# Pair 0's operands through a landing tile, key signs before the last sum, and bits first in each pair's first score tile

## The chip, the cores and the metric

The kernel runs on one core of a Trainium2 chip. The metric is the device time of one execution in microseconds (us); the median of several runs is compared. TensorE (PE) multiplies, VectorE (DVE) and ScalarE (ACT) do elementwise work, GpSimd (POOL) and SyncE (SP) mainly issue DMAs here.

## The reference

Bucketed attention over 4 batches x 8 heads, 768 positions, 64 dimensions, and then a gated feed-forward block. A query sees only keys whose six hash bits equal its own:

```python
q_bits = (np.einsum('bhsd,dk->bhsk', q, proj) > 0)      # k_bits likewise
mask = q_bucket[:, :, :, None] == k_bucket[:, :, None, :]
scores = np.where(mask, scale * np.matmul(q, k.transpose(0, 1, 3, 2)), -1000000000.0)
attn = softmax(scores)                                  # over keys, sum + 1e-09
x = matmul(attn, v)   -> (B*S, H*D)
out = (silu(x @ w_gate) * (x @ w_val)) @ w_out
```

The weights of the feed-forward block are doubles (they are read as pairs of 32-bit words); everything else is fp32.

## The kernel before

The attention stage works on 16 pairs of heads. A pair has 12 units: two halves of 384 queries by six blocks of 128 keys. For a unit, `products` (T) multiplies the transposed keys with the transposed queries of both heads in fp32, two passes each, and `mark` adds a product of bit patterns in bf16 to the same PSUM tile and then lets ScalarE take Exp of it into a ring of 12 weight tiles (A). The bit product is what masks: where two hash codes differ, the score falls far below. After the 12 units come, on TensorE, the sums of the pair before (`total`, L581), the hash products of the next pair (`hash_blocks`, L430), and `attend` (L545), which multiplies the weights with v for all 12 units. TensorE issues strictly in this written order, and so does every other engine: nothing is moved by a scheduler.

The bits of the next pair are made while this pair attends. ScalarE takes the sign of each hash product (`sign`, L435) in the order query half 0, query half 1, key half 0, key half 1; between the query and the key signs stands the copy of the row of sums (L586), which a small DMA on SP (L588) reads. `spread_q` (L447) is a DMA on the POOL queue that copies the query bits to the second head's rows. `spread_k` (L444) does the same for keys with two VectorE operations, each times a mask. Key signs and `spread_k` are put into a list `rest`, which the main loop empties at the end of the pair.

VectorE's order in a pair: the two transposes of the next pair's keys and queries (L458), then sums of the weights in `add` (L563, L567, L570 for the first half, the same for the second), then `spread_k`, the normalisation of the pair before last (L610), a reciprocal (L594) that waits for the small DMA, splits of finished outputs (L291, L296), and the conversion of feed-forward weights in pieces. A piece costs ScalarE three and VectorE five operations (L139 to L168). `PACE` says how many pieces are begun in each pair, 24 in all; the others follow in the feed-forward stage.

Pair 0 has no pair before it, so `start_first` prepares it by itself. Queries come on SP's queue and keys on ScalarE's, each in four DMAs (two heads, two halves), straight into the tile `raw`, whose rows hold both heads side by side, so that a run in memory is 64 numbers, 256 B. TensorE transposes (L468), ScalarE and VectorE copy the result out of PSUM (L472, L475). Nine matmuls with zeros (L367) keep TensorE busy until then. VectorE's copies of the hash matrix (L394) wait for two DMAs of `proj` on POOL.

PSUM is a ring of four tiles of two banks; each unit, each `joint` tile (sums and hashes) and each `av` tile takes the next one.

The feed-forward stage starts when the attention stage has issued, and takes the rest of the time.

Of the kernel before, what the change touches and what calls it, by code (L numbers as in the profile page):

```python
# [8 lines left out]
FP32 = mybir.dt.float32  # L9
# [10 lines left out]
def kernel(  # L20
# [20 lines left out]
    nc = tc.nc  # L41
    PSUM = bass.MemoryType.PSUM
    B, H, S, D = q.shape
# [37 lines left out]
    def two_banks(name):  # L81
        return pp.tile([P, 2, 512], FP32, tag="pp", name=name)
# [6 lines left out]
    def finish(todo):  # L89
        while todo:  # L90
            todo.pop(0)()
# [210 lines left out]
    def attention(scope):  # L302
# [9 lines left out]
        def fetch(n, name, queue, half=None):  # L312
            b, pr = pairs[n]
            if name == "v":
                t = raws["v", n] = raw.tile([P, 2, NCH, D], FP32, tag="vraw", name="vraw")
                queue.dma_start(
                    t.rearrange("p h c d -> p h (c d)"),
                    v[b, 2 * pr : 2 * pr + 2].rearrange("h (p c) d -> p h (c d)", c=NCH),
                )
                return  # L320
            src = q if name == "q" else k
            if not half:
                raws[name, n] = raw.tile([P, NCH, 2, D], FP32, tag=name + "raw", name=name + "raw",
                                         bufs=1)
            t = raws[name, n]
            if n == 0:
                cs = slice(half * CH, (half + 1) * CH)
                for h in range(2):
                    queue.dma_start(t[:, cs, h, :],  # L329
                                    src[b, 2 * pr + h].rearrange("(p c) d -> p c d", c=NCH)[:, cs, :])  # L330
                return
            blocks = t.rearrange("p c a b -> p (c a b)").rearrange(
                "p (c a d) -> p c a d", a=P // BLOCK, d=BLOCK)
            for h in range(2):
                for x in range(D // BLOCK):
                    at = h * D + x * BLOCK
                    queue.dma_start(
                        blocks[at : at + BLOCK],
                        src[b, 2 * pr + h][:, x * BLOCK : (x + 1) * BLOCK].rearrange(
                            "(a p c) d -> p c a d", c=NCH, p=BLOCK))  # L340

        def load(n, names):
            if n < len(pairs):
                for name in names:
                    fetch(n, name, nc.sync)

        two_proj = fixed.tile([P, NBITS], FP32, tag="proj", name="proj")
        for o in (0, D):
            nc.gpsimd.dma_start(two_proj[o : o + D, :], proj[:, :])
# [13 lines left out]
        for t in (sides["k", 0], sides["q", 0], sides["q", 1]):  # L363
            nc.vector.memset(t, 0.0)
        idle = two_banks("idle")
        for i in range(9):
            nc.tensor.matmul(idle[:, i % 2], zeros[:, 0:P], zeros[:, 0:512], start=True, stop=True)  # L367

        HR = 16
# [34 lines left out]
            twos.append(t)  # L404
        ring = [t[:, i] for t in twos for i in range(2)]

        for n, name in ((1, "k"), (1, "q"), (0, "v"), (1, "v")):
            fetch(n, name, nc.sync)
        load_words(3, nc.sync)

        T = {}
        bits = {}

# [8 lines left out]
        def front(n):  # L422
            bits["q", n] = sides["q", n % 2]
            bits["k", n] = sides["k", n % 2]
            low, high = slice(0, BLOCK), slice(D, D + BLOCK)

            def hash_blocks(todo):
                tile_ = joint(n - 2)[:, 1]
                for i, (name, half) in enumerate(todo):
                    nc.tensor.matmul(tile_[i * BLOCK : (i + 1) * BLOCK, 0:HQ], hash_w,  # L430
                                     T[name, n][:, half * HQ : (half + 1) * HQ],
                                     start=True, stop=True)

                def sign(i, name, half, to=low, **how):
                    nc.scalar.activation(bits[name, n][to, half * HQ : (half + 1) * HQ],  # L435
                                         tile_[i * BLOCK : (i + 1) * BLOCK, 0:HQ], AF.Sign,
                                         **(how or {"bias": nudge[name]}))

                return [lambda i=i, at=at, **how: sign(i, *at, **how) for i, at in enumerate(todo)]

            def spread_k(times, cols=slice(0, S)):
                b = bits["k", n][:, cols]
                for to, by in ((high, times[1]), (low, times[0])):
                    nc.vector.tensor_scalar(b[to], b[low], scalar1=by, scalar2=None, op0=ALU.mult)  # L444

            def spread_q():
                nc.gpsimd.dma_start(bits["q", n][high], bits["q", n][low])  # L447

            def hash_next(todo):
                q0, q1, *ks = hash_blocks(todo)  # L450
                q0()
                q1()
                spread_q()
                return ks + [lambda: spread_k(times_k)]

            def transpose_blocks(name):
                T[name, n] = opnd.tile([P, S], FP32, tag=name + "T", name=name + "T")
                nc.vector.transpose(T[name, n], raws[name, n].rearrange("p c h d -> p (c h d)"))  # L458

            def start_first():  # L460
                for half in range(2):
                    cols = slice(half * HQ, (half + 1) * HQ)
                    for name in "kq":
                        if not half:
                            T[name, n] = opnd.tile([P, S], FP32, tag=name + "T", name=name + "T")
                        ps = two_banks("tps")[:, 0]
                        for i in range(CH):
                            nc.tensor.transpose(ps[:, i * P : (i + 1) * P],  # L468
                                                raws[name, n][:, half * CH + i].rearrange("p h d -> p (h d)"),
                                                ident)  # L470
                        if name == "k":
                            nc.scalar.activation(T[name, n][:, cols], ps[:, 0:HQ], AF.Copy,  # L472
                                                 scale=2 / OFF)
                        else:
                            nc.vector.tensor_copy(T[name, n][:, cols], ps[:, 0:HQ])  # L475

                def both_heads(sign, name, half):
                    cols = slice(half * HQ, (half + 1) * HQ)
                    sign()
                    if name == "k":  # L480
                        spread_k(mask, cols)
                    else:
                        nc.vector.tensor_copy(bits["q", n][high, cols], bits["q", n][low, cols])

                products(0)
                todo = [("k", 0), ("q", 0), ("k", 1), ("q", 1)]
                signs = hash_blocks(todo)
                for i in range(2):
                    both_heads(signs[i], *todo[i])
                products(1)  # L490
                products(2)
                for i in range(3):
                    mark(i)
                    if i < 2:
                        both_heads(signs[2 + i], *todo[2 + i])

            order = [("q", 0), ("q", 1), ("k", 0), ("k", 1)]
            if n:
                return [lambda name=name: transpose_blocks(name) for name in "kq"] + [
                    lambda: hash_next(order)]  # L500
            return start_first()
# [10 lines left out]

        banks_of = {}

        def product(u, x, start):
            n, half, c = units[u]
            qs = slice(half * HQ, (half + 1) * HQ)
            ks = slice(c * P, (c + 1) * P)
            for h in range(2):
                rows = slice(h * D, (h + 1) * D)  # L520
                nc.tensor.matmul(banks_of[u][:, h], x["k", n][rows, ks], x["q", n][rows, qs],  # L521
                                 start=start, stop=not start)

        def products(u):
            banks_of[u] = two_banks("sc")[:, :, 0:HQ]
            product(u, T, True)

        def mark(u):
            product(u, bits, False)
            nc.scalar.activation(weights(u)[:, :, 0:HQ], banks_of.pop(u), AF.Exp,  # L530
                                 scale=SCALE * (1.0 if units[u][0] else OFF / 2))

        def score(u):
            products(u)
            mark(u)

        def attend(u):
            n, half, c = units[u]
# [84 lines left out]
                    rest.extend(f for f in steps.pop(0)() or [] if f)  # L623

        front(0)
        steps = front(1)
        last = []
        PACE = [2] * 4 + [1] * 4 + [2, 1] * 4
        splits = []
        later = []  # L630
        TURN = 5
        for n in range(len(pairs)):
# [5 lines left out]
            for i in range(2 * NCH):  # L638
                if u + i > 2:
                    score(u + i)  # L640
                if n == 0 and i == TURN:
                    prepare_pair(2)
                if i % NCH:
                    add(u + i)
                if i == (2 if n else TURN):
                    load(n + 2, "qk")
            row = total(n - 1) if n else None
            if more:
                prepare_pair(1)
            if row:  # L650
                row()
            finish(rest)
            finish(last)
            while waiting:
                last.append(waiting.pop(0)())
# [277 lines left out]
```

## Time and profile before

| what | value |
|---|---|
| median of three runs | 912.94 us (912.37 to 913.92) |
| the profiled execution | 913.47 us, span 911.4 us |
| mean granted TensorE clock | 0.999 |
| busy PE, DVE, ACT, POOL | 904.0, 666.6, 448.0, 97.0 us |
| start until the steady run of pair 0 | 0 to 13.4 us |
| attention, pairs 1 to 15 | 28.9 to 318.6 us |
| feed-forward | 318.6 to 911.4 us |
| one regular pair | 19.23 us |

The span runs from the first to the last instruction; the device time holds some 2 us more around it. All times below are from the span's start. A line of a timeline gives start, length, engine, source line, operation, what it writes and reads, shapes and count, and in brackets how long the engine had been idle and on what it waited.

### The profile page before, as it was taken

The numbers are of one execution on the slowest core, as the hardware profiler recorded it, in microseconds if no ns is written. First come the engines' busy times: TensorE is split into PE (matmuls) and PEld (weight loads), VectorE is DVE, ScalarE is ACT, GpSimd is POOL, SyncE is SP. The second block draws the span as 40 slices with busy tenths as digits, with TensorE's granted clock in tenths as the row PEclk, the third lists the DMA queues.
The fourth block names the chain that finished last, engine by engine and source line by source line (L and its number), as shares of the span: only waits on it lengthen the run. The fifth ranks groups of instructions, "written<-read, shape, count | busy, mean of one in ns | idle before, by whom it ended". The sixth has DMA issues, their size and how long they took to land.

```text
span 911.4 us, 12610 instructions
## 1 busy us (share of the span) xinstructions
PE 904.0 (99%) x4795; PEld 636.1 (70%) x4795; DVE 666.6 (73%) x774; ACT 448.0 (49%) x604; POOL 97.0 (11%) x193
## 2 busy tenths in 40 slices
PE   8999999999999999999999999999999999999998
PEld 4444444444444488888888888888888888888886
DVE  5889999989988968779785855465668754474746
ACT  6889888878888655452414243331313233413220
POOL 1111111011111120000100000101000100001000
PEclk9999999999999999999999999999999999999999
DMA  7777788787897599685756562444434642525332
GB/s 180 132 188 199 195 214 192 162 193 208 224 227 211 200 382 331 218 289 207 297 177 238 202 259 104 173 139 157 155 139 151 242 147 97 207 70 208 104 139 93
DMA packets 145579, 174.25 MB, mean 191 GB/s; under 512 B 106496, under 2 KB 115200, under 8 KB 145520
## 3 DMA queue, kind: packets, MB, share of 16 engines
q0 software_dynamic: 22864, 116.36, 36.4%
q1 hardware_dynamic: 121056, 56.71, 24.9%
q8 instruction: 38, 0.62, 0.3%
q10 hardware_dynamic: 1600, 0.39, 0.2%
q14 instruction: 21, 0.17, 0.1%
HBM read 133.17 MB, written 39.42 MB: 189 GB/s over the span
## 4 chain that ended last, share of the span: by engine, by line
PE 97%; DVE 1%; DMA 1%; ACTq 0%; issue 0%; ACT 0%; DVEq 0%
PE a L690 29%; PE o L690 22%; PE sc L521 17%; PE n L690 14%; PE av L545 13%; PE joint L581 1%; PE joint L430 1%; DMA vraw<-in_v_dram 1%; DMA kraw<-in_k_dram 0%; DVE both L567 0%; DVE both L563 0%; DVE acc L570 0%; ACTq L329 0%; DVE kb L444 0%; DVE kT L458 0%
## 5 line engine op out<-in xcount | busy, mean ns | idle before, releaser
L690 PE MATMUL a<-xparts,ring 128*128 128x512 f32 x1152 | 273.0, 389 | 0.0
L690 PEld LDWEIGHTS a<-xparts,ring 128*128 128x128 f32 x1152 | 216.1, 188 | 45.5 <-issue 0.6
L690 PE MATMUL o<-ring,hid 128*128 128x512 f32 (+1 forms) x870 | 199.1, 388 | 0.0
L690 PEld LDWEIGHTS o<-ring,hid 128*128 128x128 f32 x870 | 162.1, 188 | 35.2 <-DVE hid L745 1.0
L521 PE MATMUL sc<-qT,kT 64*128 64x384 f32 x768 | 156.9, 487 | 0.6 <-ACT A L530 0.6
L530 ACT ACTIVATE A<-sc 128x768 f32<-128x768 f32 x192 | 151.8, 815 | 7.5 <-PE sc L521 4.2
L690 PE MATMUL n<-xparts,ring 128*128 128x512 f32 x576 | 142.2, 389 | 0.0
L545 PE MATMUL av<-A,vraw 128*64 128x386 f32 (+1 forms) x768 | 127.7, 488 | 0.0
L690 PEld LDWEIGHTS n<-xparts,ring 128*128 128x128 f32 x576 | 108.1, 188 | 22.5
L735 DVE TENSOR_TENSOR v<-v,n 128x1024 f32<-128x1024 f32 x36 | 44.0, 1221 | 98.7 <-PE n L690 98.0
L248 POOL DMA_DIRECT2D ring<-ram x108 | 56.9, 529 | 499.9 <-PE n L690 328.4
L545 PEld LDWEIGHTS av<-A,vraw 128*64 128x64 f32 x768 | 53.7, 136 | 73.3 <-issue 63.4
L521 PEld LDWEIGHTS sc<-qT,kT 64*128 64x128 f32 x768 | 67.6, 187 | 48.5 <-issue 46.3
L729 ACT ACTIVATE g<-a 128x1024 f32<-128x1024 f32 x36 | 37.0, 1027 | 130.8 <-PE a L690 126.6
L740 ACT ACTIVATE hid<-v 128x1024 fp32r<-128x1024 f32 x36 | 38.2, 1062 | 114.5 <-DVE v L739 114.5
L737 ACT ACTIVATE g<-g 128x1024 f32<-128x1024 f32 x36 | 38.2, 1062 | 86.0 <-DVE g L735 86.0
L792 DVE TENSOR_TENSOR o<-o 128x512 f32<-128x512 f32 x92 | 63.0, 687 | 20.6 <-ACT o L786 18.2
L735 DVE TENSOR_TENSOR g<-g,n 128x1024 f32<-128x1024 f32 x36 | 43.8, 1217 | 32.7 <-PE n L690 32.7
L521 PE MATMUL sc<-qb,kb 64*128 64x384 bf16 x384 | 63.4, 323 | 1.1 <-DVE kb L444 1.1
L567 DVE TENSOR_TENSOR both<-both,A 128x1536 f32<-128x1536 f32 x32 | 56.2, 1757 | 3.2
L563 DVE SCALAR_TENSOR_TENSOR both<-A 128x1536 f32<-128x1536 f32 x32 | 55.7, 1741 | 3.5 <-ACT A L530 1.9
L743 DVE SCALAR_TENSOR_TENSOR hid<-hid,v 128x1024 fp32r<-128x1024 f32 x36 | 44.0, 1224 | 19.2 <-ACT hid L740 19.1
(79 smaller groups left out, 696.8 us busy)
## 6 DMA issues: line engine op xcount, KB each, us to landing
ring<-ram POOLq DMA_DIRECT2D x108, 768.0 KB, 5.1
ram<-stage POOLq DMA_DIRECT2D x23, 768.0 KB, 5.6
ram<-stage SPq DMA_DIRECT2D x13, 768.0 KB
qraw<-in_q_dram SPq DMA_DIRECT2D x64, 96.0 KB
vraw<-in_v_dram SPq DMA_DIRECT2D x16, 384.0 KB
out_dram<-o SPq DMA_DIRECT2D x23, 256.0 KB
kraw<-in_k_dram SPq DMA_DIRECT2D x60, 96.0 KB
r<-sums SPq DMA_DIRECT2D x30, 192.0 KB
```

The costliest lines, as they stand in the source:

```text
L248: nc.gpsimd.dma_start(t.bitcast(FP32), ram[at].bitcast(FP32))
L521: nc.tensor.matmul(banks_of[u][:, h], x["k", n][rows, ks], x["q", n][rows, qs], start=start, stop=not start)
L530: nc.scalar.activation(weights(u)[:, :, 0:HQ], banks_of.pop(u), AF.Exp, scale=SCALE * (1.0 if units[u][0] else OFF / 2))
L545: nc.tensor.matmul(ps[h * D : (h + 1) * D, 0:width], raws["v", n][:, h, c, :], a[:, h, 0:width], start=c == 0, stop=c == NCH - 1)
L563: nc.vector.scalar_tensor_tensor(out=t, in0=first, scalar=S * EPS / P / 2, in1=now, op0=ALU.add, op1=ALU.add)
L567: nc.vector.tensor_tensor(t, t, now, op=ALU.add)
L690: nc.tensor.matmul(ps, w, x, start=start, stop=stop)
L735: nc.vector.tensor_tensor(two(z), two(z), n_, op=ALU.subtract)
L737: nc.scalar.activation(z, z, AF.Silu)
L740: nc.scalar.activation(h, val, AF.Copy, scale=TOWARD / STEP)
L743: nc.vector.scalar_tensor_tensor(out=l, in0=h.bitcast(FP32), scalar=-STEP, in1=val, op0=ALU.mult, op1=ALU.add)
L792: nc.vector.tensor_tensor(accs[c], accs[c], t[:, 1], op=ALU.subtract)
```

## The change

Four parts.

1. Pair 0's keys and queries are loaded in memory order into a tile `landing` (runs of 768 B, both heads in one DMA, two DMAs each in place of four) and copied from there to the `raw` tiles, keys by ScalarE and queries by VectorE, in front of the transposes. The landing tile takes the place in memory of `both`, which is used first later. Seven idle matmuls stand where nine stood.
2. The loads of pair 1, of the first two v tiles and of three weight pieces stand after `front(0)` in the code instead of ahead of it, in the same order on SP.
3. All four signs and both spreads go into `rest`, keys first. The main loop runs the first three of them (two key signs and `spread_k`) ahead of the pair's last `add`, then that `add`, then the query signs and `spread_q`, and only then the row copy.
4. In the first unit of pairs 1 to 15 the bit product opens the PSUM tile and the fp32 product closes it. In all other units the order stays. `PACE` is 2 in pairs 0 to 2, 1 in pairs 3 to 7, then 2, 1, 2, 1, 2, 2, 2, 1 (before: 2 in pairs 0 to 3, 1 in 4 to 7, then 2, 1 four times).

```diff
             if n == 0:
-                cs = slice(half * CH, (half + 1) * CH)
-                for h in range(2):
-                    queue.dma_start(t[:, cs, h, :],
-                                    src[b, 2 * pr + h].rearrange("(p c) d -> p c d", c=NCH)[:, cs, :])
+                at = slice(half * CH * D, (half + 1) * CH * D)
+                queue.dma_start(
+                    landing[name].rearrange("p h c d -> p h (c d)")[:, :, at],
+                    src[b, 2 * pr : 2 * pr + 2].rearrange("h (p c) d -> p h (c d)", c=NCH)[:, :, at])
                 return
...
+        room = att.tile([P, 2, 2, HQ], FP32, tag="both", name="landing", bufs=1)
+        landing = {name: room[:, i].rearrange("p x q -> p (x q)").rearrange(
+            "p (h c d) -> p h c d", h=2, d=D) for i, name in enumerate("qk")}
...
-        for i in range(9):
+        for i in range(7):
             nc.tensor.matmul(idle[:, i % 2], zeros[:, 0:P], zeros[:, 0:512], start=True, stop=True)
...
             def hash_next(todo):
-                q0, q1, *ks = hash_blocks(todo)
-                q0()
-                q1()
-                spread_q()
-                return ks + [lambda: spread_k(times_k)]
+                q0, q1, k0, k1 = hash_blocks(todo)
+                return [k0, k1, lambda: spread_k(times_k), q0, q1, spread_q]
...
+                        here = slice(half * CH, (half + 1) * CH)
+                        (nc.scalar.copy if name == "k" else nc.vector.tensor_copy)(
+                            raws[name, n].rearrange("p c h d -> p h c d")[:, :, here],
+                            landing[name][:, :, here])
                         ps = two_banks("tps")[:, 0]
...
         def score(u):
-            products(u)
-            mark(u)
+            if u % (2 * NCH):
+                products(u)
+                mark(u)
+            else:
+                banks_of[u] = two_banks("sc")[:, :, 0:HQ]
+                product(u, bits, True, False)
+                product(u, T, False, True)
+                mark(u, False)
...
-        PACE = [2] * 4 + [1] * 4 + [2, 1] * 4
+        PACE = [2] * 3 + [1] * 5 + [2, 1] * 2 + [2] * 3 + [1]
...
-                if i % NCH:
+                if i % NCH and i < 2 * NCH - 1:
                     add(u + i)
...
             if more:
                 prepare_pair(1)
+            for _ in range(3):
+                if rest:
+                    rest.pop(0)()
+            add(u + 2 * NCH - 1)
+            finish(rest)
             if row:
                 row()
-            finish(rest)
             finish(last)
```

More of the change, by code (lines that the diff above doesn't have):

```diff
@@ L405, in attention @@
         ring = [t[:, i] for t in twos for i in range(2)]
-        for n, name in ((1, "k"), (1, "q"), (0, "v"), (1, "v")):
-            fetch(n, name, nc.sync)
-        load_words(3, nc.sync)
         T = {}
@@ L513, in attention, with product @@
         banks_of = {}
-        def product(u, x, start):
+        def product(u, x, start, stop):
             n, half, c = units[u]
@@ L521, in product, with mark @@
                 nc.tensor.matmul(banks_of[u][:, h], x["k", n][rows, ks], x["q", n][rows, qs],
-                                 start=start, stop=not start)
+                                 start=start, stop=stop)
         def products(u):
             banks_of[u] = two_banks("sc")[:, :, 0:HQ]
-            product(u, T, True)
-        def mark(u):
-            product(u, bits, False)
+            product(u, T, True, False)
+        def mark(u, last=True):
+            if last:
+                product(u, bits, False, True)
             nc.scalar.activation(weights(u)[:, :, 0:HQ], banks_of.pop(u), AF.Exp,
@@ L625, in attention @@
         front(0)
+        for n, name in ((1, "k"), (1, "q"), (0, "v"), (1, "v")):
+            fetch(n, name, nc.sync)
+        load_words(3, nc.sync)
         steps = front(1)
         last = []
-        PACE = [2] * 4 + [1] * 4 + [2, 1] * 4
+        PACE = [2] * 3 + [1] * 5 + [2, 1] * 2 + [2] * 3 + [1]
         splits = []
```

## The prediction

> **What bounds the kernel now.** I read the busy shares first, then the table by stage, the chain of waits, and last the timelines of three places where the chain leaves TensorE or loses time on it: one pair opening, the one long stall, and the start.
>
> The page's first part, then the table of stages (start to end, length, busy time of PE, PEld, DVE, ACT, POOL, clock, DMA):
>
> ```profile
> PE 904.0 (99%) x4795; PEld 636.1 (70%) x4795; DVE 666.6 (73%) x774; ACT 448.0 (49%) x604; POOL 97.0 (11%) x193
> ...
> 0.00:13.40 13.40, 10.48 (x53) 4.43 (x53) 5.17 (x16) 5.59 (x8) 2.71 (x23) 1.00 0.58 105
> 28.90:318.56 289.66, 288.93 (x2041) 138.19 (x2041) 263.63 (x315) 237.85 (x362) 37.41 (x62) 1.00 0.78 197
> 318.56:911.40 592.84, 589.08 (x2599) 486.31 (x2598) 384.73 (x431) 192.40 (x216) 56.38 (x107) 1.00 0.53 189
> ```
>
> TensorE is the bound everywhere except in the first 13.4 us. The feed-forward stage (592.84 us) is not touched by the change. So what can be won is in 0 to 13.4 and in the gaps of 0.73 us in 28.9 to 318.6, plus what a busy PE hides: matmuls that issue later than they could.
>
> The chain of waits (start, length, what) shows a regular pair of 19.23 us (9.89 scores, about 1.4 sums and hashes, 7.91 attend) and one irregular place:
>
> ```profile
> 67.36 9.89 PE sc L521 x72
> 78.68 7.91 PE av L545 x48
> 86.59 3.43 PE sc L521 x24
> 90.01 4.79 DMA vraw<-in_v_dram
> 97.11 1.65 DVE both L563
> 98.85 1.77 DVE both L567
> 100.72 0.97 DVE acc L570
> 101.78 1.77 DVE both L563
> 103.64 1.77 DVE both L567
> 107.50 9.22 PE sc L521 x68
> ```
>
> From the opening at 86.52 to the one at 145.29, three pairs, it is 58.77 us where 3 x 19.23 = 57.69 would do, so 1.08 us is lost around pair 5. The timeline of VectorE and TensorE there says on what:
>
> ```profile
> 103.64 1.76 DVE L567 TENSOR_TENSOR both<-both,A 128x1536 f32<-128x1536 f32 x1
> 105.51 0.96 DVE L570 TENSOR_TENSOR acc<-both 128x768 f32<-128x768 f32 x1
> 106.50 0.85 DVE L444 TENSOR_SCALAR kb<-kb,columns 32x768 bf16<-32x768 bf16 x2
> ...
> 107.50 0.34 PE L521 MATMUL sc<-qb,kb 64*128 64x384 bf16 x2 [0.73 <-DVE kb L444]
> ```
>
> The spreading of the key signs (L444) stands behind the last sum of the pair (L567, L570), and in this pair VectorE is late.
>
> A regular opening and the unit after it (TensorE's timeline, pair 2):
>
> ```profile
> 48.06 0.92 PE L521 MATMUL sc<-qT,kT 64*128 64x384 f32 x4
> 48.81 0.33 PE L521 MATMUL sc<-qb,kb 64*128 64x384 bf16 x2
> 48.97 0.81 PE L521 MATMUL sc<-qT,kT 64*128 64x384 f32 x4
> 49.62 0.33 PE L521 MATMUL sc<-qb,kb 64*128 64x384 bf16 x2
> ```
>
> A later unit takes 0.81 us (48.97 to 49.78); the first takes 0.91[...].
>
> The start (TensorE's and VectorE's timelines):
>
> ```profile
> 5.76 0.17 DVE L394 COPY hash<-proj 64x6 f32<-64x6 f32 x1 [0.64 <-DMA proj<-in_proj_dram]
> ...
> 6.62 0.52 PE L468 MATMUL tps<-ident,kraw 128*128 128x128 f32 x3 [0.65 <-DMA kraw<-in_k_dram]
> 7.40 0.92 PE L521 MATMUL sc<-qT,kT 64*128 64x384 f32 x4
> ```
>
> The second half of the keys holds the transposes to 6.62, and the first scores issue at 7.40. From there to 13.33 everything is one chain of hash, signs, spread, Exp, so a shift at 7.40 reaches the end in full.
>
> [...]94 ns for kb against 187 for kT. [...]the idle matmuls issue 0.43 us apart for 512 columns, while later 384 columns take 0.16. [...]the trace has 421 ns for 512 elements from SBUF (L153) and 558 for 384 from PSUM (L475). [...]the packet records here take 18 ns for 256 B, 46 for 1024 B, 65 for 1536 B.
>
> **The change part by part.**
>
> *Opening with bits.* In pairs 1 to 15 the first unit issues bits, T, T instead of T, T, bits. Today the first T pass takes 48.06 to 48.48, 0.42 us where later ones take 0.32: 105 ns of exposed loading. Bits that came after a stall (107.50) were followed by T at 107.66, 0.16 to 0.17 where 0.16 is regular: some 10 ns exposed. Gain 15 x 0.095 = 1.43 us. Unit 1's T then follows T, whose pass of 0.32 hides a load of 0.19. Bounds: 1.2 if half the exposure of a fast load shows, 1.5 if none.
>
> *Key signs ahead of the last sum.* L444 moves in front of L567 and L570, so it comes 1.86 + 0.99 = 2.85 us sooner when VectorE is late. In pair 4 it would end near 104.5, before the opening at 105.85, and the 1.08 us go. The price is that VectorE waits for the key signs where it is early: they leave ScalarE 12.64 us after the opening (first sign at 11.46, two of 0.59), against 11.1 for the end of the second L563. So the last sum ends some 1.2 us later in pairs 1 and 2 (38.12 + 1.86 = 39.98, signs at 41.5). Behind it are L610, the reciprocal, the pieces and the next transposes. In pair 3 the lag meets one piece less (PACE 1 for 2: 0.42 + 0.69 + 0.69 = 1.8 us), and the later pairs run at 18.0 us of VectorE work (13.1 of rows that every pair has, 3.1 for one piece, 1.8 for a split) per 19.1. I walked this through all pairs with these rows: L444 ends 2.5 to 5 us before each opening, the transposes before each hash; at the end two pieces in pair 13 add 3.1 us of VectorE, and the sums of pair 15 still end about 1.7 us before their total. Cost 0; up to 1.5 if that last slack is wrong.
>
> *Query signs last.* Their DMA (L447, POOL) is issued after both key signs, 1.18 us later, and with bits first it is needed 0.75 sooner. Its landing:
>
> ```profile
> DMA to landing us min/median/max: 2.1/3.6/5.3
> ```
>
> Taken one by one (issue plus landing plus 1.18 against the opening): pair 5, 99.53 + 4.9 + 1.18 = 105.6 against 105.85; pair 6, 119.66 + 5.3 + 1.18 = 126.1 against 125.99; pair 13, 0.65 us spare; the rest 0.9 to 3.0. Cost 0.1, bounds 0 and 0.6. The row copy (L586) also goes 1.2 us later, but the few DMA behind it on SP waits for key loads in nearly every pair anyway (row done at 61.2, reciprocal at 66.5).
>
> *Landing tile.* Keys and queries of pair 0 come in 768 B runs, 4 DMAs for 8. Packets: 3072 x 18 ns / 16 = 3.5 us before; 1024 at about 37 ns (between 18 and 46) / 16 = 2.4 after, and the bytes are the same, so the second halves land about 1.1 us sooner, near 5.4 for 6.5. Added: two ScalarE copies (between 0.48 of L586 and 0.67 of L139; 0.55) and two VectorE copies. No row shows that copy; 0.25 (L483, bf16) to 0.56 (L475, PSUM); by L153 less 128 elements, 0.36. The VectorE copies stand behind the two hash copies (L394), which wait for proj, today to 5.76. With t for that moment: query copy t + 0.13 to 0.49, transposes to t + 1.1, qT to 1.69, second copy to 1.99, transposes from 2.05, scores at t + 2.49. Equal to today's 7.40 at t = 4.91. The second proj DMA was issued at 1.91 and shares the engines with the 3072 packets; with fewer I take t = 5.2 (between 4.9, close behind the first at 4.96, and 5.76 unchanged): cost 0.3, bounds 0 and 0.85, plus 0.4 if the copy runs at the slow rate; and a gain of up to 0.6 if proj lands at 4.3. ScalarE's side ends earlier: copy by 4.6, kT by 5.6, second copy by 6.2, its transposes by 6.8, before the second query ones.
>
> *Two idle matmuls less.* They end at 4.28 for 5.14. Cost 0 if the clock still opens near 5.1.
>
> *Fetches after front(0), PACE.* The pair-1 loads still wait for the transposes (kraw issued at 7.18); 24 pieces in both. 0.
>
> Sum: -1.43 - 1.08 + 0.1 + 0.3 = -2.11. The profiled execution took 913.47 us (span 911.40), 0.53 above the median 912.94; it becomes 911.36, and the median 910.8.
>
> **The rivals.**
>
> 1. *The start eats the gain.* proj unchanged at 5.76 and slow copies: +0.85 to +1.25, total -1.2 to -1.6: 911.5. For: VectorE's order puts proj in front. Against: less traffic. Chance 0.13.
> 2. *The start gains.* t near 4.3: total -3.0: 909.9. Chance 0.14.
> 3. [...]Only 3.0 us of idle matmuls, then a gap while the query copy waits; transposes, first scores and hashes (about 0.33 + 0.33 + 0.85 + 0.65 us) would take twice that: +2.2, about 913.0.[...] Chance 0.07.
> 4. *Slower: query bits late at every opening.* If L447's landing grows by x, the pairs pay what exceeds their slack. By the list above x = 0.9 costs 2.1 and cancels the gain; x = 1.5 costs 5.3, giving 916. For: the landing already varies from 2.1 to 5.3, and POOL's DMA now starts beside VectorE's last sum. Against: same engines and traffic. Chance 0.18.
>
> **How the numbers follow.** The forecast's own case has 0.48, 910.2 to 911.5. About 0.2%, 1.8 us, is what a measurement of this kernel can tell from no change, so the border is 911.1: seven tenths of the own case and rival 2 lie below (0.34 + 0.14 = 0.48); the rest of the own case, rivals 1 and 3 and a little of 4 are within (0.14 + 0.13 + 0.07 + 0.02 = 0.36); rival 4 gives slower 0.16. The range leaves out most of rival 4 and the best of rival 2: 909.6 to 913.5.
>
> **What would show it.** Right: unit 0 of a pair takes 0.82 us; no wait of TensorE on L444 around 105; a pair is 19.13 us; first scores near 7.7. Wrong: openings that wait for the qb DMA, a start beyond 8.2, or a score matmul at half clock after 6 us; any of these adds up to more than the 2.1 us.

## The result, and the profile after

| | median us | runs |
|---|---|---|
| before | 912.54 | 5 (912.09 to 913.92) |
| after | 927.49 | 5 (926.38 to 928.38) |

The ratio is 1.0162, 95% interval 1.0147 to 1.0177. The change costs 1.6%, 14.8 us by the ratio, where 910.8 us were forecast. The profiled execution took 927.25 us, its span 925.5 (before: 913.47 and 911.4).

The chain of waits of the changed kernel first, in a stretch of regular pairs (start, length, what):

```profile
88.82 9.80 PE sc L521 x72
98.62 0.78 PE joint L588 x8
99.40 0.65 PE joint L429 x8
100.05 7.91 PE av L552 x48
107.96 9.80 PE sc L521 x72
```

From 88.82 to 107.96 is one pair: 19.14 us for 19.23, with 9.80 us of scores for 9.89. No step of VectorE stands in this part of the chain any more. So two parts of the change do what they were meant to do. TensorE's and VectorE's timelines of the same place:

```profile
107.89 0.34 PE L521 MATMUL sc<-qb,kb 64*128 64x384 bf16 x2
108.06 1.45 PE L521 MATMUL sc<-qT,kT 64*128 64x384 f32 x8
```

```profile
103.53 0.86 DVE L443 TENSOR_SCALAR kb<-kb,columns 32x768 bf16<-32x768 bf16 x2
104.31 1.74 DVE L574 TENSOR_TENSOR both<-both,A 128x1536 f32<-128x1536 f32 x1
```

The bits open without a wait, the first fp32 product follows 0.17 us after them, and the key bits are spread at 103.53, ahead of the last sum.

The loss is elsewhere. The table by stage (start to end, length, busy time of PE, PEld, DVE, ACT, POOL, clock, DMA share, GB/s):

```profile
0.00:15.90 15.90, 11.62 (x51) 4.39 (x51) 5.80 (x18) 6.47 (x10) 2.72 (x23) 0.89 0.55 119
31.42:280.10 248.68, 248.68 (x1768) 118.68 (x1768) 224.97 (x270) 207.08 (x314) 29.50 (x49) 1.00 0.77 192
280.10:332.40 52.30, 43.24 (x274) 20.04 (x272) 38.01 (x46) 30.93 (x48) 8.00 (x13) 0.90 0.51 182
332.40:925.50 593.10, 589.12 (x2602) 486.43 (x2598) 384.67 (x431) 192.44 (x216) 56.39 (x107) 1.00 0.53 189
```

Row two is 13 pairs in which TensorE is busy all the time. The feed-forward stage is 593.1 us as before. Rows one and three hold the loss. The start ends 2.5 us later (the fourth unit's bits issue at 15.85 for 13.33). The stretch of the last two pairs takes 52.3 us, where the same stretch of before took 38.6:

```profile
279.90:318.49 38.59, 38.59 (x274) 18.30 (x272) 35.53 (x43) 29.76 (x45) 6.66 (x11) 1.00 0.65 223
```

Of the 13.7 us between them TensorE stands idle for 9.1; in the other 4.6 it is busy with the same 274 matmuls, at a mean clock of 0.90. With 1.3 us won by the openings of the 13 pairs and 1.0 by the stall that is gone, the sum is 2.5 - 2.3 + 13.7 + 0.2 for the tail = 14.1, the difference of the spans.

What TensorE waits for in row three, on its timeline:

```profile
288.32 1.65 PE L521 MATMUL sc<-qT,kT 64*128 64x384 f32 x4 [5.62 <-ACT xT L559]
312.56 1.65 PE L521 MATMUL sc<-qT,kT 64*128 64x384 f32 x4 [3.43 <-ACT xT L559]
```

Both stalls fall at the opening of a pair (14 and 15). xT is ScalarE's copy of the finished output out of PSUM (0.79 us); the page's row of these matmuls has 9.1 us of waiting for it in the whole execution, and these two are all of it. ScalarE's timeline tells why it is late here:

```profile
276.75 0.69 ACT L140 ACTIVATE words<-words 128x512 int32<-128x512 uint16 x1
286.31 0.66 ACT L139 ACTIVATE stage<-words 128x512 f32<-128x512 f32 x1 [8.87 <-DMA ram<-stage]
...
287.48 0.79 ACT L559 COPY xT<-av 128x768 f32<-128x768 f32 x1
```

In front of the copy stands L139, the first step of a piece of feed-forward weights, and it waits 8.87 us for a DMA. In before the same engine at the same place goes through:

```profile
280.01 0.17 ACT L551 ACTIVATE e<-av 128x1 f32<-128x1 f32 x1 [2.83 <-PE av L545]
280.08 0.79 ACT L552 COPY xT<-av 128x768 f32<-128x768 f32 x1
```

There ScalarE waits for TensorE, as it should. The chain of waits of the changed kernel gives the DMA's own history:

```profile
275.92 3.15 DMA few<-row
279.10 0.23 DVE few L601
...
279.90 0.69 DVE stage L168
...
281.16 5.04 DMA ram<-stage
...
286.31 0.66 ACT stage L139
...
287.58 0.69 ACT xT L559
```

VectorE finishes an older piece (L168) in this very pair, behind a reciprocal that waits for a small DMA, and the write-out of that piece lands at 286.20. Only then is its tile free for L139.

The reason lies in how the tiles are shared. `stage` tiles are two in turn, and a tile holds two pieces, 2k and 2k+1. Pieces begun in pair n are scaled by ScalarE in pair n, but written out by VectorE's steps in pair n+1, and in the code ScalarE's part of a pair (`begin_pieces`) stands ahead of VectorE's (`advance_pieces`). An even piece i opens a new tile; that tile last held pieces i-4 and i-3. So piece i-3 has to be begun in pair n-2 at the latest. The old `PACE` keeps to this everywhere. The new one begins 19 and 20 in pair 13 and 21 and 22 in pair 14, while 17 was begun in pair 12 and 19 in pair 13: pieces 20 and 22 break the rule, and the stalls are at the openings that follow pairs 13 and 14.

The start, on VectorE's and TensorE's timelines:

```profile
5.53 0.36 DVE L397 COPY hash<-proj 64x6 f32<-64x6 f32 x2 [1.10 <-DMA proj<-in_proj_dram]
5.92 0.36 DVE L463 COPY qraw<-landing 128x384 f32<-128x384 f32 x1
```

```profile
6.34 0.55 PE L468 MATMUL tps<-ident,qraw 128*128 128x128 f32 x3 [0.99 <-DVE qraw L463]
7.89 0.88 PE L468 MATMUL tps<-ident,qraw 128*128 128x128 f32 x3 [0.68 <-DVE qraw L463]
8.70 1.65 PE L521 MATMUL sc<-qT,kT 64*128 64x384 f32 x4
```

The hash copies wait for `proj` and are done at 5.89; the query copy stands behind them. Then three transposes take 0.88 us where three took 0.55, and four score matmuls 1.65 for 0.92: the clock is at half from 7.89 to 11.30.

### The profile page after: what moved, and what is told of

Its sections match the earlier page's. It is cut to its first block, busy times and chain, and to the rows that moved or that the text cites. A ratio compares the mean times of both kernels' runs of the same rounds, so it can differ in the third digit from the quotient of the medians.

```text
span 925.5 us, 12551 instructions
## 1 busy us (share of the span) xinstructions
PE 908.2 (98%) x4793; PEld 636.8 (69%) x4793; DVE 666.6 (72%) x776; ACT 449.3 (49%) x606; POOL 97.1 (10%) x193
## 4 chain that ended last, share of the span: by engine, by line
PE 95%; DMA 1%; ACT 1%; issue 1%; DVE 1%; DVEq 0%; ACTq 0%; POOLq 0%
PE a L704 28%; PE o L704 21%; PE sc L521 17%; PE n L704 14%; PE av L552 12%; PE joint L588 1%; PE joint L429 1%; DMA ram<-stage 1%; DMA proj<-in_proj_dram 0%; DMA few<-row 0%; ACT kb L434 0%; ACT stage L139 0%; ACT words L140 0%; DVE kb L443 0%; PE tps L468 0%
## 5 line engine op out<-in xcount | busy, mean ns | idle before, releaser
L521 PEld LDWEIGHTS sc<-qT,kT 64*128 64x128 f32 x768 | 70.0, 192 | 52.9 <-issue 34.0
```

## The experiments

Twelve kernels, in three groups, each beside runs of before of its own (medians 913.16, 913.01 and 912.34 us). A ratio is to these, and so kernels of two groups are best compared by their ratios; differences of medians are named as such. Theory S says that the turn-over of the stage tiles (their reuse for later pieces) makes the two stalls, L that too many pieces late in the stage do.

**1. a_regroup: the changed kernel, pieces shared out to tiles one place later from piece 9 on.** `PACE`, and with it the work of every engine in every pair, stays.

```diff
-        if i // 2 not in stages:
-            stages[i // 2] = stagep.tile([P, 2, 3, PIECE], FP32, tag="stage", name="stage")
-        staged[i] = st = stages[i // 2][:, i % 2]
+        at = i if i < 9 else i + 1
+        if at // 2 not in stages:
+            stages[at // 2] = stagep.tile([P, 2, 3, PIECE], FP32, tag="stage", name="stage")
+        staged[i] = st = stages[at // 2][:, at % 2]
```

> The changed kernel with its own PACE; only the grouping of the weight pieces two to a stage tile is moved by one from piece 8 on, so that no tile's two pieces begin in different pairs where PACE is 2, 2, 2. Theory S (the stalls at the openings of pairs 14 and 15 come from a stage tile shared by two pieces that were begun in different pairs: ScalarE's L139 waits for a write-out that VectorE can only issue in the same pair): both stalls go, 927.5 - 13.9 = 913.6. Theory L (three pairs with two pieces each in a row are too much work or traffic for VectorE and the DMAs): nothing changes, about 927.

914.51 us, 1.0009 (1.0002 to 1.0016), by the medians 13 us less than the changed kernel. The chain of waits has no step off TensorE where the stalls were:

```profile
272.26 7.91 PE av L553 x48
280.17 9.79 PE sc L522 x72
...
291.39 7.91 PE av L553 x48
299.31 9.82 PE sc L522 x72
```

The same pieces are begun in the same pairs, so S holds and L falls. The expectation asks that both pieces of a tile begin in one pair. The rule above asks for less, and is the one that counts: the old `PACE` begins 14 in pair 9 and 15 in pair 10, in one tile, and has no stall.

**2. b_pace_only: before, with the new `PACE` alone.**

```diff
-        PACE = [2] * 4 + [1] * 4 + [2, 1] * 4
+        PACE = [2] * 3 + [1] * 5 + [2, 1] * 2 + [2] * 3 + [1]
```

> The kernel before with the PACE of the changed kernel alone. Theory S: the two stalls appear here as well, some 13.9 us, less the 1.1 us of pair 5 if the piece less in pair 3 takes VectorE's lag away: 925.3. Rival (the stalls need the later signs and sums of the changed order as well): 912 to 915.

922.87 us, 1.0108 (1.0094 to 1.0122), 2.4 us under the 925.3 expected. One line of constants costs about 9.9 us of the 14.8. TensorE's timeline:

```profile
284.89 0.92 PE L521 MATMUL sc<-qT,kT 64*128 64x384 f32 x4 [3.53 <-ACT xT L552]
308.89 0.92 PE L521 MATMUL sc<-qT,kT 64*128 64x384 f32 x4 [2.80 <-ACT xT L552]
```

Both stalls are there without any other part of the change, but shorter than 5.62 and 3.43. In the changed kernel the small DMA ahead of the reciprocal leaves SP, behind the key loads, 6.8 us before the opening is due (275.92 against 288.32 - 5.62 = 282.70), here 8.0 us (273.38 against 281.36). That is 1.2 us of the 2.1 between the first stalls; the small DMA itself (3.15 us for 2.42) and the write-out (5.04 for 4.74) make up the rest. What is late ahead of a write-out adds to its stall.

**3. a_pace_aligned: the changed kernel with a third `PACE`, which keeps the rule.**

```diff
-        PACE = [2] * 3 + [1] * 5 + [2, 1] * 2 + [2] * 3 + [1]
+        PACE = [2] * 3 + [1] * 6 + [2, 1, 1] + [2] * 4
```

> The changed kernel with PACE 2 x 3, 1 x 6, 2, 1, 1, 2 x 4: 24 pieces as before, four pairs with two pieces in a row at the end, but from an even count, so that both pieces of a stage tile begin in one pair. Theory S: no stall, about 913.6. Theory L: more late pieces than in the changed kernel, so the stalls stay or grow, 927 or more.

915.21 us, 1.0025 (1.0013 to 1.0036), every pair 19.13 or 19.14 us. Four pairs of two pieces in a row at the end do no harm; what its profile has to show for being slower than before is the start, where four score matmuls take 1.65 us for 0.92 (at 9.07, half clock), and a wait of 1.35 us for feed-forward weights at 332.11 (see 9).

**4. one_stall: the rule broken once.** The changed kernel with the start of before, tiles shared as at first, and the last four counts in another order.

```diff
-        PACE = [2] * 3 + [1] * 5 + [2, 1] * 2 + [2] * 3 + [1]
+        PACE = [2] * 3 + [1] * 5 + [2, 1] * 2 + [2, 2, 1, 2]
```

> Base is start_back_regroup (910.8 us: changed kernel, start of before, regrouped stage tiles). Two edits: the grouping of pieces in stage tiles goes back to 2k, 2k+1, and the last four counts of PACE are 2, 2, 1, 2 instead of 2, 2, 2, 1. The rule of theory S (an even piece i begun in pair n needs piece i-3 begun in pair n-2 or before) is then broken once, by piece 20 in pair 13, and kept by piece 22, which is begun in pair 15. S: one stall, at the opening of pair 14, and none at that of pair 15; 910.8 + 5.5 to 7.3 = 916.3 to 918.1. Rival (L: three pairs with two pieces late in the stage are too much for ScalarE or the DMA queues, wherever a tile turns over): either both stalls stay, about 922, or none, about 911.

919.45 us (916.85 to 921.17), 1.0069 (1.0051 to 1.0087): 8.6 us over start_back_regroup (kernel 8) by the ratios, more than the 5.5 to 7.3 expected. TensorE at the opening of pair 14, and the chain from pair 15 on:

```profile
285.45 1.65 PE L514 MATMUL sc<-qT,kT 64*128 64x384 f32 x4 [5.58 <-ACT xT L552]
```

```profile
305.15 9.80 PE sc L514 x72
314.95 0.78 PE joint L581 x8
315.73 7.91 PE av L545 x48
```

One violation, one stall, at the place that the rule names. Its idle time is that of the changed kernel's first stall; in its profile the clock stays at half for 6.83 us behind it (284.36 to 291.19), not for 3.41, which fits the higher cost.

**5. b_open_only: before, with the bits first at the opening.** `product` and `mark` take what they need for it.

```diff
         def score(u):
-            products(u)
-            mark(u)
+            if u % (2 * NCH):
+                products(u)
+                mark(u)
+            else:
+                banks_of[u] = two_banks("sc")[:, :, 0:HQ]
+                product(u, bits, True, False)
+                product(u, T, False, True)
+                mark(u, False)
```

> The kernel before with the opening of each pair by bits alone. If the 105 ns of exposed fp32 weight load per opening go: 15 x 0.095 = 1.4 us, of which pair 5 loses up to 0.8 again, because the bits that come late there are now wanted 0.75 us sooner, and pair 6 as much: net 0 to -1.4, about -0.4. Rival (the fast weights are as exposed as the slow ones): +0.5 to +1.5.

911.75 us, 0.9988 (0.9981 to 0.9994), or -1.1 us (-1.7 to -0.5). Its late openings on TensorE's timeline:

```profile
105.87 0.34 PE L521 MATMUL sc<-qb,kb 64*128 64x384 bf16 x2 [0.67 <-DVE kb L444]
125.93 0.34 PE L521 MATMUL sc<-qb,kb 64*128 64x384 bf16 x2 [0.85 <-DVE kb L444]
```

A pair that is shorter, and bits that are needed first, make more of the old wait for the key bits: 1.5 us here, 1.1 in before. It eats a part of the gain.

**6. b_signs_only: before, with the key signs first and ahead of the last sum.** 
```diff
+                q0, q1, k0, k1 = hash_blocks(todo)
+                return [k0, k1, lambda: spread_k(times_k), q0, q1, spread_q]
...
+            for _ in range(3):
+                if rest:
+                    rest.pop(0)()
+            add(u + 2 * NCH - 1)
+            finish(rest)
```

> Before, with the order of the signs of the changed kernel alone: key signs and their spread ahead of the query's, and three steps ahead of the last sum. The prediction took 1.08 us for it (the two late openings of before, pairs 5 and 6). Theory 1: these stalls are in every run, 913.0 - 1.1 = 911.9. Theory 2: the profiled run of before has more of them than most runs, or the hash that now comes later opens a wait of its own: 912.4 to 913.0.

912.22 us, 0.9995 (0.9987 to 1.0003): -0.5 us, with zero inside the interval. In its profile all fourteen intervals between openings are 19.23 us, so no opening is late. That it gains less than the 1.1 us which the profile of before showed fits a profile of before that had more of the stall than most runs; those weren't profiled. The next kernel shows how much this varies.

**7. ab_start_pace_back: the changed kernel with start and `PACE` of before.** The landing tile and its copies go; 5 and 6 together stay, and the place of the fetches.

```diff
-        for i in range(7):
+        for i in range(9):
...
-        PACE = [2] * 3 + [1] * 5 + [2, 1] * 2 + [2] * 3 + [1]
+        PACE = [2] * 4 + [1] * 4 + [2, 1] * 4
```

> The changed kernel with the start of before (direct loads, nine idle matmuls) and the PACE of before; what remains is bits first, the key signs ahead of the last sum, and the place of the fetches. If the start (+2.5) and PACE (+13.9) are all that costs: 912.5 - 1.4 - 1.1 = 910.0. Rival (the late query bits or ScalarE's new order cost something that the stalls hide): 911 to 913.

910.61 us, 0.9973 (0.9967 to 0.998): -2.5 us (-3.0 to -1.8), the fastest median of all, better than both kernels. Its profiled execution took 912.42, 1.8 above its median, and lost 2.2 us in pairs 4 and 5 (19.67 and 20.77 us for 19.13). The largest of these waits, on TensorE's timeline:

```profile
117.65 0.52 PE L426 MATMUL joint<-qT,hash 128*32 128x384 f32 x2 [0.83 <-DVE qT L451]
```

Nineteen of its twenty other runs are faster than the profiled one, by 1.2 us or more. So VectorE's lateness in these pairs probably differs between executions of one kernel; a single profile gives its place, not its size.

**8. start_back_regroup: the same with the new `PACE`, regrouped by the edit of 1.**

```diff
-        PACE = [2] * 4 + [1] * 4 + [2, 1] * 4
+        PACE = [2] * 3 + [1] * 5 + [2, 1] * 2 + [2] * 3 + [1]
```

> The changed kernel with the regrouped stage tiles and with the start of before (direct loads, nine idle matmuls); its own PACE. If the changed PACE is sound once the stage tiles fit it, it saves what the old PACE still cost with the new order (hash products waiting for late transposes in pairs 4 and 5, 0.5 + 1.0, and bits in pair 5, 0.5): 910.6 - 2.0 = 908.6. Rival: no gain over the old PACE, 910.6. Against the run with the regrouped tiles and the landing tile it gives the cost of the new start alone: 2.5 expected from the two profiles, so 912.

910.77 us, 0.9975 (0.9964 to 0.9986). The profile has no waits in pairs 4 to 6, but the median is that of 7. The new `PACE`, once its stalls are taken away, is worth nothing that can be measured.

**9. b_landing_only: before, with the landing tile, seven idle matmuls and the moved fetches.**

```diff
+                        here = slice(half * CH, (half + 1) * CH)
+                        (nc.scalar.copy if name == "k" else nc.vector.tensor_copy)(
+                            raws[name, n].rearrange("p c h d -> p h c d")[:, :, here],
+                            landing[name][:, :, here])
```

> Before, with the start of the changed kernel alone (landing tile, 7 idle matmuls, fetches after the first pair's front). Theory F (the loss of the start doesn't depend on the other parts): as a_regroup against start_back_regroup, 914.5 - 910.8 = 3.7, so 913.0 + 3.7 = 916.7, with scores beginning near 8.7 us and a wait of about 1 us for the first expert weights near 331 us. Rival: only the start itself belongs to the landing tile, 913.0 + 2.5 = 915.5, and no wait for the expert weights.

914.78 us, 1.0025 (1.0017 to 1.0033), or +2.3 us (+1.6 to +3.0). That is the rival's 915.5 rather than theory F's 916.7, and there is no wait for the first feed-forward (expert) weights. In the changed kernel the start costs 3.1 us by the ratios of 1 and 8 (1.0009 - 0.9975 = 0.0034), which is no clear difference from 2.3, given the intervals. In the profile of 1, 1.0 us is a wait for feed-forward weights (ring) at 330.71. Kernels 3, 10 and 11 have it too (1.35, 1.18 and 0.39 us); 12, this one, the changed kernel itself and all with the start of before have not. In the four that wait, POOL issues the last pair's load 2.5 to 3.4 us after the stage's first matmul, in 7, 8, 12 and this one 1.0 to 1.8 us after it; in the chain of 1 VectorE's last piece stands ahead of it. So the wait goes with a late VectorE. What makes VectorE late there is open; the landing tile by itself doesn't.

Five of the 14 runs lie between 913.29 and 913.59, the other nine between 914.17 and 917.06. In the profiled one, at 913.5, three transposes take 0.87 us at 4.79 and 0.55 at 6.32, and those that follow run at full clock. TensorE's timeline reads:

```profile
7.87 0.52 PE L471 MATMUL tps<-ident,qraw 128*128 128x128 f32 x3 [0.68 <-DVE qraw L466]
8.32 0.92 PE L524 MATMUL sc<-qT,kT 64*128 64x384 f32 x4
```

So the start has two losses: scores at 8.32 for 7.40, 0.9 us, from the late query copy, and half clock on top, as in the profiles of 1 and 3 (four score matmuls in 1.65 us, at 8.70 and 9.07). That half clock is what sets the nine slower runs apart is likely, but none of them was profiled.

**10. a_regroup_warm: 1 with idle matmuls in the gaps.** Eight in front, four behind the first and three behind the second key transposes.

```diff
-        for i in range(7):
-            nc.tensor.matmul(idle[:, i % 2], zeros[:, 0:P], zeros[:, 0:512], start=True, stop=True)
+        keep_busy(8)
...
+                        if name == "k":
+                            keep_busy(4 - half)
```

> The regrouped changed kernel with its landing tile, and 15 idle matmuls in place of 7: 8 ahead, 4 behind the first key transposes, 3 behind the second. Theory C (of the 2.5 us that the start is late, 1.6 are first scores and hashes at half clock[...]): the clock stays open and the time falls by 1.6, to 912.9. Theory Q (only the query copy's wait for proj counts): no gain, or up to 1 us lost to the idle matmuls.

912.72 us, 0.9995 (0.9987 to 1.0003), against 1 -1.8 us by the medians and -1.3 by the ratios. In its profile, of the slowest of its runs (914.08), three transposes take 0.87 us at 4.86 and 0.54 at 7.23, and the first four score matmuls 0.92 us where 1 has 1.65, though they come later, at 9.23 for 8.70. More work gives less time: as nothing else was changed, what it saves is time at half clock.

**11. a_regroup_hash: 1 with the hash copies behind the second query copy.**

```diff
-        for h in range(2):
-            rows = slice(h * D, (h + 1) * D)
-            nc.vector.tensor_copy(hash_w[rows, h * HR : h * HR + NBITS], two_proj[rows, :])
...
+                        if half and name == "q":
+                            fill_hash()
```

> The regrouped changed kernel with its landing tile; the two copies of the hash matrix, which wait for proj, stand behind the second query copy on VectorE instead of in front of the first. Theory Q: the query transposes follow the key transposes at 5.1 instead of 6.3, first scores near 7.2 for 8.7, 1.5 us gained, and more if the clock then stays open. Theory C alone: the clock closes the same way, at most 0.5 us gained.

911.70 us, 0.9991 (0.9983 to 1.0), against 1 -2.8 us by the medians and -1.6 by the ratios (two of its 20 runs are above 916). VectorE's timeline:

```profile
4.37 0.31 DVE L467 COPY qraw<-landing 128x384 f32<-128x384 f32 x1
...
7.02 0.36 DVE L400 COPY hash<-proj 64x6 f32<-64x6 f32 x2
```

The copy of the first query half begins at 4.37, 1.55 us before the changed kernel's. The first scores come at 8.05 for 8.70, not near the 7.2 expected: the transposes ahead of them take 0.84 to 0.90 us for three, and the four score matmuls 1.65 us, at half clock.

**12. a_regroup_hash_fill: 11 with four more idle matmuls.** Eight in front, two behind the first query and one behind the second key transposes.

```diff
+                        keep_busy({("q", 0): 2, ("k", 1): 1}.get((name, half), 0))
```

> a_regroup_hash (911.7), with 8 idle matmuls ahead of the first transposes, 2 behind the first query transposes and 1 behind the second key transposes, so that the clock stays open. Theory: the two losses of the start, late query copy and clock, add: 1.8 of a_regroup_warm was the clock, of which a_regroup_hash still has part in some runs (its profile: clock opened at 10.25); first scores at 8.0 to 8.2 at full clock, 910.7 to 911.2. Rival: in most runs of a_regroup_hash the clock is open anyway, so 911.5 to 911.9.

911.87 us, 0.9991 (0.9984 to 0.9997), no better than 11, so the two gains don't add; the rival is right. What changes is the spread: none of the 21 runs is above 912.81. The profile begins its scores at 7.73, at full clock (four in 0.92 us), 0.75 us after those of start_back_regroup (6.98). Even the best start with a landing tile found here, that of 11 and 12, is 1.5 us behind the old one by the ratios (0.9991 for 0.9975).

## Why the prediction failed

**The step that failed** is "Fetches after front(0), PACE": "24 pieces in both. 0." The count of pieces was right, and it was not what matters. Which pair a piece is begun in decides whether its tile is still waiting for its write-out; kernel 2 measures this at +9.9 us (1.0108) by itself, and kernel 1 takes 14.0 us by the ratios (1.0162 - 1.0009) off the changed kernel by touching nothing else. The prediction walked VectorE through all pairs, pieces included, and left out ScalarE's wait for the tile, which blocks everything behind it on that engine. No rival named it; rival 4, the only one that ends slower, put the lateness on the query bits.

**The start** was taken at +0.3, with bounds 0 and 0.85; alone it is +2.3. Two terms were off. t, the start of the second hash copy, is 5.72 and not 5.2, hardly before the 5.76 of before, which is rival 1's case (chance 0.13); so the query copy begins at 5.92. With this t the prediction's own sum, t + 2.49, gives first scores at 8.21, and kernel 9, at full clock, has them at 8.32. And "Cost 0 if the clock still opens near 5.1" met a clock that opened at 4.48 and fell back at 7.89. Rival 3 described the half clock (+2.2, in transposes, scores and hashes), with a chance of 0.07. The copy itself, 0.36 us, was right, and the queries had landed by then (11 copies them from 4.37 on without a wait). For "first scores near 7.7" it was 8.70; "a start beyond 8.2" and "a score matmul at half clock after 6 us" were the text's own signs that it is wrong.

**Opening with bits**: -1.43 was taken; the profile confirms the size at each opening (9.80 us of scores for 9.89), and alone it measures -1.1, within its interval. Of the cause of the longer first pass in before, the trace shows this much: the load of its weights (187 ns for kT; kb takes 94) starts together with it, at 48.06, and in the next unit 0.16 us ahead of the pass (48.81 for 48.97).

**Key signs ahead of the last sum**: the mechanism is right, and no opening waits. The size, -1.08, was read from one execution; alone it measures -0.5 (-1.2 to +0.3). Both together were put at -2.51 + 0.1 and measure -2.5 (kernel 7). That is more than the -1.6 of the two alone, though within the intervals, and it fits: 6 takes away the stall that 5 makes larger (1.5 us for 1.1).

**Query bits late** (rival 4): no opening of the changed kernel waits for them, and their DMA lands sooner than before (median 2.6 us for 3.6). The wait does occur in kernel 7: in its profile one such DMA holds the bits of an opening for 0.28 us (at 106.19), within the bounds of 0 and 0.6.

Put together, kernel 7 gives -2.5, the start +3.1, the tiles +14.0: +14.6 for 14.8 measured. This closes almost by construction, as start and tiles are differences on the way from 8 to the changed kernel; the only free check in it is that 7 and 8 agree. The four parts, each alone on before, give less: -1.1 - 0.5 + 2.3 + 9.9 = +10.6. The 4.2 us that are missing lie mostly in the stalls: 9.05 us idle in the changed kernel for 6.33 in kernel 2, and half clock behind them for 10.24 us for 6.82, an estimated 1.7 us lost (half of the difference).

## What to carry to other kernels

Where two buffers are used in turn and one buffer serves two steps, a list of "how many when" is a list of waits: write down, for each step that opens a buffer, when its last user is released, and which engine's queue is blocked meanwhile. A change of constants needs the same walk as a change of code. And a loss at the start or in a stall is not only its idle time: look at the clock records for what follows it.

## What the runs showed of the hardware

The clock records in the traces of before and of the changed kernel hold two values, 1.0 and 0.5. In before's trace the clock is at 1.0 from 5.17 to 909.70. In the changed kernel's it is at 1.0 from 4.48 on, but for 7.89 to 11.30, 287.78 to 291.20 and 311.68 to 318.50 (3.41, 3.41 and 6.83 us), where it is at 0.5. Ahead of a trace's first clock record the views give 1.00 whatever the clock: kernel 3 has a mean of 1.000, though its first score matmuls take 1.65 us for 0.92. Stretches of the changed kernel next to these changes (columns as in the table by stage):

```profile
4.48:7.89 3.41, 1.41 (x10) 0.97 (x10) 1.52 (x5) 1.59 (x4) 0.00 (x0) 1.00 0.03 7
7.89:11.30 3.41, 3.41 (x15) 1.18 (x15) 0.56 (x1) 0.00 (x0) 0.00 (x0) 0.50 0.58 92
280.96:284.37 3.41, 1.74 (x14) 0.70 (x10) 2.65 (x5) 0.00 (x0) 1.38 (x3) 1.00 0.61 187
284.37:287.78 3.41, 0.00 (x0) 0.00 (x0) 0.75 (x2) 1.47 (x4) 0.52 (x1) 1.00 1.03 380
287.78:291.20 3.42, 2.88 (x10) 1.47 (x12) 2.84 (x5) 3.36 (x5) 1.30 (x2) 0.50 0.92 299
308.27:311.68 3.41, 0.86 (x8) 0.18 (x4) 1.13 (x3) 1.13 (x3) 0.80 (x2) 1.00 1.03 324
311.68:315.09 3.41, 2.53 (x10) 1.45 (x12) 1.39 (x2) 3.41 (x7) 1.30 (x2) 0.50 0.83 309
```

In the 3.41 us ahead of the three falls TensorE was busy for 1.41, 0.00 and 0.86 us. In the first 3.41 us at half clock it was busy for 3.41, 2.88 and 2.53 us; after the first two the clock was at 1.0 again, after the third it stayed at 0.5 for 3.41 us more, and so the second stall costs twice as much half clock as the first. Other stretches of the same length were not followed by a fall: 280.96 to 284.37 here, with 1.74 us of PE, and 5.17 to 8.58 in before, with 2.76.

The kind of work gives no clear picture either. At the start the stretch ahead of the fall held transposes alone, 1.41 us of them. In b_landing_only 2.07 us of PE between 5.52 and 8.93, of which only the last 0.6 were scores, were not followed by half clock: its hash products at 9.17 take 0.51 us, where the changed kernel's at 10.28 take 0.85. In kernel 2, 1.30 us of scores alone between 282.78 and 286.19 were followed by 3.41 us at half clock. What brings a fall and what ends it isn't settled by these runs.
